# Quarter-array products and a planner with new durations in a fused attention kernel

## The chip, the core and the metric

The kernel runs on one core of a Trainium2 chip. The metric is the device time of one execution in microseconds (us); times are medians of several executions, and the profile is of one execution. The engines are named as in the profile: PE is TensorE (its weight loads are PEld), DVE is VectorE, ACT is ScalarE, POOL is GpSimd, SP is SyncE.

## The reference

One block of multi-head attention, in bfloat16: 2048 rows, 448 columns, 16 heads of 28 columns.

```python
B, S, D, H = 1, 2048, 448, 16          # x: (B,S,D), wqkv: (D,3D), wo: (D,D)
Dh = D // H                            # 28
qkv = (x @ wqkv).reshape(B, S, 3, H, Dh).transpose(2, 0, 3, 1, 4)
q, k, v = qkv[0], qkv[1], qkv[2]
scores = jnp.einsum("bhqd,bhkd->bhqk", q, k) * (Dh ** -0.5)
p = softmax(scores, axis=-1)
o = jnp.einsum("bhqk,bhkd->bhqd", p, v)
return o.transpose(0, 2, 1, 3).reshape(B, S, D) @ wo
```

## The kernel before

**Tiles.** The heads form four groups (`g`) of four; each head takes 32 of the 128 partitions (28 of its own, the rest for a softmax bound, the sums and padding). The queries form four chunks (`c`) of 512 columns. One pair of group and chunk is a set; there are 16. In a set, each of the 4 heads has 16 key tiles of 128 keys, so 64 half-steps: scores of one head, one key tile and 512 queries. There are 1024 half-steps in all.

**What one half-step does.** TensorE makes the scores from 32 (or, zero padded, 64) rows (L678, "S"; row tiles of the array, `32*128` or `64*128` in the profile), into one half of a PSUM pair `a0`/`a1` or into a single bank `d0`, `d1` or `m`. Pairs go to ScalarE, whose exponential covers two half-steps at once (128x1024, L864, `pt<-a`). Single ones go to VectorE, which makes the exponential by integer arithmetic (L879, `I<-d`), and for every four of them two further terms (L902, `J<-I`). TensorE then multiplies with V: products of 128 rows by 32 columns, one for each head, four of them side by side in the four column strips of the array (L962, `128*32`). Four such quarters are called a wave here. A half-step of ScalarE needs one quarter, one of VectorE three. All quarters of a set accumulate in the bank `o`, which VectorE copies out (L991); the sums are inverted and spread by DMAs, and GpSimd multiplies (L1013).

**The side work of TensorE.** Projections of K and Q are made in quarters of 32 columns too (L270, `112*32`). The rest uses the whole array: the norms of K and Q behind the softmax bound (L314, L477: `sq` times a mask, 512 columns), the projection of V (L513: 224 columns, four contraction chunks for each half-job), the output projection (L547, L1146 for the last chunk, L1213 at the very end: 448 columns), and products with zeros that fill idle time (L708 into the open bank `o`, L711 into a free bank). All but the last set's outputs pass through the bank `m`, which VectorE empties.

**The planner.** The order of instructions on each engine is made in Python when the program is built. The planner keeps a time for each engine, always advances the engine that is earliest, and picks its next piece of work by rules (`pick_pe`, `pick_act`, `pick_dve` and so on), with durations that are written in the code. On the chip every engine then takes its list in order and waits where data or a bank is not there. What matters here:

- `do_s` emits the scores for the next exponential as soon as their PSUM pair is free, with up to two single half-steps for VectorE; `do_sd` emits single half-steps alone.
- `s_deadline` is the time by which the next scores must begin so that ScalarE does not wait; other work of TensorE (`do_pv` for waves, the jobs of `add("PE", ...)`, `dense` for zero products) is picked only if it ends by then, with 0.1 us of tolerance.
- `D_S` is the duration of scores, `D_WAVE` of a wave, `D_SWITCH` a charge for each piece of other work; `D_EXP` is the duration of an exponential. `LATS` and `LAT` are the latencies from engine to engine. `SLOW_V` stretches all durations of VectorE by 3%.
- `dve_ok` decides whether a half-step goes to VectorE, by comparing when VectorE would be done with when ScalarE would be.

```python
D_S = 0.325
D_WAVE = 0.2135
D_SWITCH = 0.11
D_EXP = 0.912
# dense(): a zero product
return t + D_SWITCH + D_WAVE
# do_pv(): one or two waves
end = t + D_SWITCH + D_WAVE * len(ws)
```

Of the kernel before, what the change touches and what calls it, by code (L numbers as in the profile page):

```python
# [17 lines left out]
LATS = {("ACT", "PE"): 0.32, ("PE", "ACT"): 0.12, ("PE", "DVE"): 0.15, ("DVE", "PE"): 0.2}  # L18
D_S = 0.325
D_WAVE = 0.2135  # L20
D_SWITCH = 0.11
D_EXP = 0.912
SLOW_V = 1.03
D_SOON = 0.0
URGENT = 100
S_LEAD = 0.44


class Op:
    def __init__(self, eng, dur, emit, need=(), gives=(), pri=0, acq=None, rel=None, gate=0, lag=0.0, land=0.0,  # L30
                 cols=0, port=False):
        self.eng, self.dur, self.emit = eng, dur * (SLOW_V if eng == "DVE" else 1.0), emit
        self.need, self.gives, self.pri = list(need), list(gives), pri
        self.acq, self.rel, self.gate, self.lag, self.land, self.cols, self.port = acq, rel, gate, lag, land, cols, port
# [3 lines left out]
def kernel(  # L38
# [178 lines left out]
    cur = {"s": 0, "u": 0, "o": None, "oset": 0, "pv": 0, "half": 0, "o_open": False}  # L217
# [24 lines left out]
    def run(op, t):  # L242
# [3 lines left out]
        end = t + op.dur  # L246
        if op.port:
            port[op.eng] = end
# [4 lines left out]
        if isinstance(op.rel, tuple):  # L253
            parts.setdefault(op.rel[0], []).append(end + LAT)
            if len(parts[op.rel[0]]) == op.rel[1]:
                res[op.rel[0]] = max(parts.pop(op.rel[0]))
        elif op.rel is not None:
            res[op.rel] = end + LAT
# [6 lines left out]
    def mm_proj(ps, t, g, c, ccs):  # L265
        for cc in ccs:
            for i in range(HG):
# [4 lines left out]
                                 tile_position=(0, HP * i))  # L272

# [12 lines left out]
    def k_job(g, sc, bank, pri, gate=0, split=2):  # L286
# [14 lines left out]
        for p in range(split):  # L301
            add("PE", n * D_WAVE + (D_SWITCH if split > 1 else 0.02), lambda p=p: mm(p), pri=pri, gate=gate, cols=448 * n,
# [3 lines left out]
        add("POOL", 1.05, lambda: square(key, KAt[(g, sc)][:]), need=[key], gives=[("ksq", g, sc)], pri=pri, port=True)  # L306

    def kn_job(g, bank, pri, gate=0):
        key = ("KN", g)

        def mm(sc):
            if sc == 0:
                held[key] = bank_tile(bank) if bank[0] != "a" else pair_tile(bank)
            nc.tensor.matmul(out=held[key][:, 0:QW], lhsT=maskK[:, sc, :], rhs=sqt.pop(("K", g, sc))[:],  # L314
                             start=(sc == 0), stop=(sc == NQC - 1))
# [13 lines left out]
        for sc in range(NQC):  # L329
            add("PE", D_WAVE + 0.05, lambda sc=sc: mm(sc), pri=pri, gate=gate, cols=512,  # L330
# [5 lines left out]
    def k_first(sc, bank, nbank, eng, sq_eng, pri, late=False):  # L336
# [47 lines left out]
        add("PE", CC * D_WAVE + 0.02, mm, pri=pri, cols=448 * CC, acq=bank,  # L384
# [16 lines left out]
    def q_job(g, c, bank, pri, gate=0, split=2):  # L401
# [25 lines left out]
        for p in range(split):  # L427
            add("PE", n * D_WAVE + (D_SWITCH if split > 1 else 0.02), lambda p=p: mm(p), pri=pri, gate=gate, cols=448 * n,
# [7 lines left out]
        else:  # L436
            add("POOL", 1.05, lambda: square(key, QAt[(g, c)][:]), need=[key], gives=[("qsq", g, c)], pri=pri, port=True)
# [33 lines left out]
    def qn_job(g, cs, bank, pri, gate=0):  # L471
        key = ("QN", g, cs[0])

        def mm(k):
            if k == 0:
                held[key] = bank_tile(bank)
            nc.tensor.matmul(out=held[key][:], lhsT=maskK[:, cs[k], :], rhs=sqt.pop(("Q", g, cs[k]))[:],  # L477
                             start=(k == 0), stop=(k == len(cs) - 1))
# [16 lines left out]
        for k in range(len(cs)):  # L495
            add("PE", D_WAVE + 0.05, lambda k=k: mm(k), pri=pri, gate=gate, cols=512,
                need=[("qsq", g, cs[k]), ("km", g)] + ([key + (k - 1,)] if k else []), gives=[key + (k,)],
                acq=bank if k == 0 else None)
        add("DVE", 0.94, bound, need=[key + (len(cs) - 1,)], gives=[("su",) + key], rel=bank, pri=pri, port=True)
# [3 lines left out]
    def v_job(h, kt, bank, pri, gate=0, eng="DVE"):  # L503
# [4 lines left out]
        def mm(part):  # L508
# [3 lines left out]
            for cc in range(CC):  # L512
                nc.tensor.matmul(out=held[key][:, part * w:(part + 1) * w], lhsT=XT[b][cc // 2][:, cc % 2, t * P:(t + 1) * P],  # L513
                                 rhs=WRAW[2][:, cc, h * w:(h + 1) * w], start=(cc == 0), stop=(cc == CC - 1))
# [9 lines left out]
        for p in range(2):  # L524
            add("PE", 4 * 0.105 + D_SWITCH, lambda p=p: mm(p), pri=pri, gate=gate, cols=4 * 196,
# [14 lines left out]
    def oproj_job(c, tq, pri):  # L540
        key = ("O", c, tq)

        def mm(part):
            if part == 0:
                held[key] = bank_tile("m")
            for g in (2 * part, 2 * part + 1):
                nc.tensor.matmul(out=held[key][:, 0:D], lhsT=otile(g, c)[:, tq * P:(tq + 1) * P], rhs=WO[:, g, :],  # L547
                                 start=(g == 0), stop=(g == G - 1))
# [8 lines left out]
        for p in range(2):  # L557
            add("PE", 2 * 0.19 + D_SWITCH, lambda p=p: mm(p), pri=pri, cols=2 * D,
                need=[("OT", g, c) for g in range(G)] + ([key + (p - 1,)] if p else []), gives=[key + (p,)],
                acq="m" if p == 0 else None)  # L560
        add("DVE", 0.56, evac, need=[key + (1,)], gives=[key], rel="m", pri=pri)
# [144 lines left out]
    def dense(t, to):  # L706
        if to == "o" and cur["o_open"]:
            nc.tensor.matmul(out=cur["o"][:], lhsT=zero[:, 0:P], rhs=zero[:], start=False, stop=False,  # L708
                             skip_group_check=True)
# [3 lines left out]
        return t + D_SWITCH + D_WAVE  # L713
# [66 lines left out]
    def put_d(got):  # L780
        end = 0.0
        for b, pd, step, ch, n, t in got:
            end = max(end, t + D_S)
# [44 lines left out]
    def s_deadline():  # L828
# [3 lines left out]
        if len(exps) == 0:  # L832
            return max(r, free["ACT"] - S_LEAD)
        nxt = max(free["ACT"], exps[0][0]) + D_EXP * len(exps)
        return max(r, nxt - S_LEAD)

    def do_s(t):
# [16 lines left out]
        res[bank] = None  # L854
        end = t + D_S
# [20 lines left out]
    def do_a(t):  # L876
# [3 lines left out]
        end = t + 0.6 * SLOW_V  # L880
        res[b] = end + LAT
# [3 lines left out]
        pending.append({"step": step, "k": 0, "ap": dst.bitcast(BF16), "ready": end + LAT, "pt": None, "ch": ch})  # L885
# [12 lines left out]
    def do_add(t):  # L898
# [4 lines left out]
        end = port["DVE"] = t + (m * QW * 0.00026 + 0.068) * SLOW_V  # L903
        for n in range(m):
            pending.append({"step": ch["steps"][n], "k": k, "ap": r[:, n * QW:(n + 1) * QW].bitcast(BF16),
                            "ready": end + LAT, "pt": None, "ch": ch})
# [38 lines left out]
    def do_pv(t, ws):  # L945
# [7 lines left out]
        end = t + D_SWITCH + D_WAVE * len(ws)  # L953
# [25 lines left out]
    def finish_set(s, end):  # L979
# [37 lines left out]
        add("DVE", 0.26, recip, need=[("den", s)], gives=[("rec", s)], pri=50, port=True)  # L1017
# [30 lines left out]
    def pick_pe(t):  # L1048
# [8 lines left out]
        if main and left() and t + D_S + 0.1 <= dl:  # L1057
# [8 lines left out]
        ws = full[:2]  # L1066
        if len(ws) < 2 and (last_chance or op is None):
            ws = ws + rest[:2 - len(ws)] if last_chance else ws
        backlog = len(full)
        d_pv = D_SWITCH + D_WAVE * len(ws)  # L1070
        pv_ok = ws and (len(ws) >= 2 or last_chance) and t + d_pv <= dl + 0.1
# [189 lines left out]
```

## Time and profile before

| what | value |
|---|---|
| median of 3 executions | 370.25 us (370.12 to 370.31) |
| the profiled execution's own time | 370.24 us |
| its span, first to last instruction | 368.4 us |
| granted TensorE clock, mean | 0.999 |
| busy PE, DVE, ACT | 349.5, 347.3, 350.4 us |
| first exponential starts, last one ends | 19.08 us, 359.8 us |

Busy time is the union of the recorded instructions of an engine. Products are pipelined and the record of one goes on after the next has begun, so start-to-start times tell more than durations. The granted clock is given in tenths for 40 slices of the span (PEclk). "Idle before" is the time in which an engine had nothing running, with who ended it behind the arrow.

### The profile page before, as it was taken

Reading aid. Unit: us, or ns where it says so; the run is one execution under the profiler, and the core shown is the slowest. Engines: PE = TensorE matmul, PEld = TensorE weight load, DVE = VectorE, ACT = ScalarE, POOL = GpSimd, SP = SyncE. Lnnn points to the kernel's source line nnn. Section 1 sums busy time; section 2 is a strip of 40 time slices with the busy share of each in tenths; the row PEclk is TensorE's granted clock in tenths of the full one; section 3 lists DMA queues with packets and bytes.
Section 4 is the critical chain, followed back from the end, with each engine's and each line's share of the span. In section 5 each row is a group of like instructions: output and inputs, shape, how many; then the busy total and the mean of one; then the engine's idle time right before and its main releaser. Section 6 shows DMA issues by size and latency. Waiting matters only on the chain.

```text
span 368.4 us, 8926 instructions
## 1 busy us (share of the span) xinstructions
PE 349.5 (95%) x3522; PEld 111.6 (30%) x3522; DVE 347.3 (94%) x632; ACT 350.4 (95%) x384; POOL 72.7 (20%) x95
## 2 busy tenths in 40 slices
PE   8899999999999999999999999998898999999995
PEld 4443322222333233232222222222222222222222
DVE  7799999998999999999999999999999999999973
ACT  4599999999999999999999999999999999999991
POOL 8931033242010511221011314201010101010010
PEclk9999999999999999999999999999999999999999
DMA  8510010011001000010000002100000001010101
GB/s 254 126 39 12 3 29 31 8 41 36 6 29 32 2 4 28 22 52 16 29 3 9 23 4 59 24 16 18 24 8 10 25 27 55 26 56 27 42 16 50
DMA packets 15058, 12.18 MB, mean 33 GB/s; under 512 B 6812, under 2 KB 13096, under 8 KB 15016
## 3 DMA queue, kind: packets, MB, share of 16 engines
q1 hardware_dynamic: 13464, 10.19, 9.7%
q10 hardware_dynamic: 1040, 1.02, 0.9%
q8 instruction: 27, 0.44, 0.5%
q0 software_dynamic: 512, 0.40, 0.5%
q14 instruction: 15, 0.12, 0.1%
HBM read 7.58 MB, written 1.96 MB: 26 GB/s over the span
## 4 chain that ended last, share of the span: by engine, by line
PE 52%; ACT 30%; DVE 10%; issue 6%; DVEq 0%; ACTq 0%
ACT pt L864 30%; PE a L678 19%; PE o L962 16%; PE m L270 7%; DVE I L879 4%; DVE J L902 4%; PE m L547 1%; PE m L513 1%; PE o L595 1%; PE o L708 1%; PE d L678 1%; PE m L314 1%; DVE osb L552 1%; PE d L573 1%; PE a L270 1%
## 5 line engine op out<-in xcount | busy, mean ns | idle before, releaser
L864 ACT ACTIVATE pt<-a 128x1024 bf16<-128x1024 f32 x368 | 339.2, 1125 | 1.1 <-PE a L678 0.4
L879 DVE TENSOR_SCALAR I<-d 128x512 int16<-128x512 f32 x260 | 170.1, 682 | 5.3 <-PE d L678 3.9
L678 PE MATMUL a<-QP,KA 32*128 32x512 bf16 (+1 forms) x726 | 141.6, 381 | 11.2 <-ACT pt L864 10.1
L962 PE MATMUL o<-pt,VA 128*32 128x512 bf16 x736 | 105.5, 385 | 0.0
L902 DVE TENSOR_SCALAR J<-I 128x2048 int16<-128x2048 int16 x144 | 102.5, 744 | 0.2
L678 PEld LDWEIGHTS <-KA 32*128 32x128 bf16 (+1 forms) x1024 | 48.5, 91 | 145.4 <-issue 144.5
L678 PE MATMUL d<-QP,KA 32*128 32x512 bf16 x256 | 84.0, 384 | 0.4 <-DVE I L879 0.3
L962 PE MATMUL o<-J,VS 128*32 128x512 bf16 x576 | 78.7, 385 | 0.4 <-DVE J L902 0.4
L962 PE MATMUL o<-I,VA 128*32 128x512 bf16 x288 | 66.3, 386 | 0.1
L1013 POOL TENSOR_TENSOR xs<-o_sb,rr 128x512 bf16<-128x512 f32 x12 | 16.6, 1382 | 103.3 <-DMA rr<-scr 87.0
L962 PEld LDWEIGHTS <-VA 128*32 128x32 bf16 x1024 | 24.2, 94 | 36.7 <-issue 36.3
L280 POOL TENSOR_TENSOR sq<-QA 128x512 bf16<-128x512 bf16 x15 | 18.3, 1219 | 60.9 <-DVE QA L420 60.9
L270 PE MATMUL m<-XT,WRAW 112*32 112x512 bf16 x384 | 29.5, 384 | 0.0
L280 POOL TENSOR_TENSOR sq<-KA 128x512 bf16<-128x512 bf16 x12 | 13.2, 1102 | 59.2 <-DVE KA L298 59.2
L962 PEld LDWEIGHTS <-VS 128*32 128x32 bf16 x576 | 18.1, 94 | 19.7 <-issue 19.7
L879 DVE TENSOR_SCALAR I<-m 128x512 int16<-128x512 f32 x28 | 19.0, 679 | 0.1
L513 PE MATMUL m<-WRAW,XT 112*128 112x224 bf16 x128 | 17.1, 261 | 0.2
L1013 POOL TENSOR_TENSOR OTL<-o_sb,rr 128x512 bf16<-128x512 f32 x3 | 4.1, 1367 | 56.3 <-DMA rr<-scr 56.3
L708 PE MATMUL o<-zero 128*128 128x512 bf16 x40 | 13.5, 386 | 0.0
L513 PEld LDWEIGHTS <-XT 112*128 112x128 bf16 x128 | 10.2, 97 | 7.1 <-issue 7.1
L991 DVE COPY o_sb<-o 128x512 f32<-128x512 f32 x15 | 10.3, 684 | 1.4 <-PE o L962 1.3
L547 PE MATMUL m<-WO,xs 128*128 128x448 bf16 x36 | 10.9, 358 | 0.3 <-DVE I L879 0.2
(119 smaller groups left out, 195.8 us busy)
## 6 DMA issues: line engine op xcount, KB each, us to landing
rr<-scr SPq DMA_DIRECT2D x15, 256.0 KB
QP<-QA SPq DMA_DIRECT2D x60, 28.0 KB
out_dram<-osb SPq DMA_DIRECT2D x12, 112.0 KB
WRAW<-in_wqkv_dram SPq DMA_DIRECT2D x3, 392.0 KB
xs<-in_x_dram ACTq DMA_DIRECT2D x4, 224.0 KB
xs<-in_x_dram SPq DMA_DIRECT2D x4, 224.0 KB
QP<-su SPq DMA_DIRECT2D x30, 2.0 KB
out_dram<-VS SPq DMA_DIRECT2D x2, 224.0 KB
```

The source lines that it names most:

```text
L270: nc.tensor.matmul(out=ps[HP * i:HP * (i + 1), :], lhsT=w[:, cc, h * Dh:h * Dh + HP], rhs=XT[c][cc // 2][:, cc % 2, :], start=(cc == 0), s ...
L280: nc.gpsimd.tensor_tensor(out=t[:], in0=src, in1=src, op=ALU.mult)
L513: nc.tensor.matmul(out=held[key][:, part * w:(part + 1) * w], lhsT=XT[b][cc // 2][:, cc % 2, t * P:(t + 1) * P], rhs=WRAW[2][:, cc, h * w: ...
L547: nc.tensor.matmul(out=held[key][:, 0:D], lhsT=otile(g, c)[:, tq * P:(tq + 1) * P], rhs=WO[:, g, :], start=(g == 0), stop=(g == G - 1))
L678: nc.tensor.matmul(out=out_ap, lhsT=KAt[(g, j // XB)][r, (j % XB) * P:(j % XB + 1) * P], rhs=q[r, :], start=True, stop=True, tile_position ...
L708: nc.tensor.matmul(out=cur["o"][:], lhsT=zero[:, 0:P], rhs=zero[:], start=False, stop=False, skip_group_check=True)
L864: nc.scalar.activation(out=pt[:], in_=ps[:], func=ACT.Exp, scale=LN2 / 128.0)
L879: nc.vector.tensor_scalar(out=dst, in0=pd[:], scalar1=BIAS, scalar2=0.0, op0=ALU.add, op1=ALU.max)
L902: nc.vector.tensor_scalar(out=r[:, w], in0=ch["I"][:, w], scalar1=float(SHIFT[k]), scalar2=None, op0=ALU.add)
L962: nc.tensor.matmul(out=o[HP * i:HP * (i + 1), :], lhsT=vt[:, j % XB, gg, HP * i:HP * (i + 1)], rhs=e["ap"], start=(SETMM[key] == 1), stop= ...
L991: nc.vector.tensor_copy(out=st["o_sb"][:], in_=o[:])
L1013: nc.gpsimd.tensor_tensor(out=otile(g, c), in0=st["o_sb"][:], in1=st["rr"][:], op=ALU.mult)
```

## The change

A new helper makes a product over the whole array as four quarters, each with 32 of the 128 weight columns, at the four column strips. It is used for the norms in `kn_job` and `qn_job`, the projections of V, all output projections, and the zero product into the open bank `o`. The transposes, the norms of the first group (`k_first`, `qn_first`) and the zero product into a free bank stay as they were.

The planner's numbers are replaced, the charge `D_SWITCH` is gone, and a turn is charged in its place: scores begin at the earliest `D_TURN` after the last product in column form (`cur["c_end"]`). Waves are picked one at a time instead of two. The 3% on VectorE is gone, and the latency to TensorE after a release is taken from `LATS`.

```diff
-LATS = {("ACT", "PE"): 0.32, ("PE", "ACT"): 0.12, ("PE", "DVE"): 0.15, ("DVE", "PE"): 0.2}
-D_S = 0.325
-D_WAVE = 0.2135
-D_SWITCH = 0.11
-D_EXP = 0.912
-SLOW_V = 1.03
+LATS = {("ACT", "PE"): 0.165, ("PE", "ACT"): 0.167, ("PE", "DVE"): 0.13, ("DVE", "PE"): 0.145}
+D_S = 0.323
+D_TURN = 0.143
+D_WAVE = 0.226
+D_EXP = 0.904
+TOL = 0.1
-S_LEAD = 0.44
+S_LEAD = 0.49
...
+    def quarters(out, lhsT, rhs, start, stop, **k):
+        for i in range(P // HP):
+            r = slice(HP * i, HP * (i + 1))
+            nc.tensor.matmul(out=out[r, :], lhsT=lhsT[:, r], rhs=rhs, start=start, stop=stop, tile_position=(0, HP * i), **k)
...
# qn_job (kn_job, v_job, oproj_job, early_jobs and the last products alike)
-            nc.tensor.matmul(out=held[key][:], lhsT=maskK[:, cs[k], :], rhs=sqt.pop(("Q", g, cs[k]))[:],
-                             start=(k == 0), stop=(k == len(cs) - 1))
+            quarters(held[key][:], maskK[:, cs[k], :], sqt.pop(("Q", g, cs[k]))[:], k == 0, k == len(cs) - 1)
...
# durations of the jobs
-            add("PE", D_WAVE + 0.05, lambda k=k: mm(k), pri=pri, gate=gate, cols=512,
+            add("PE", D_WAVE, lambda k=k: mm(k), pri=pri, gate=gate, cols=512,
-            add("PE", 4 * 0.105 + D_SWITCH, lambda p=p: mm(p), pri=pri, gate=gate, cols=4 * 196,
+            add("PE", 4 * 0.1, lambda p=p: mm(p), pri=pri, gate=gate, cols=4 * 196,
-            add("PE", 2 * 0.19 + D_SWITCH, lambda p=p: mm(p), pri=pri, cols=2 * D,
+            add("PE", 2 * 0.192, lambda p=p: mm(p), pri=pri, cols=2 * D,
...
# dense: zero products
-            nc.tensor.matmul(out=cur["o"][:], lhsT=zero[:, 0:P], rhs=zero[:], start=False, stop=False,
-                             skip_group_check=True)
+            quarters(cur["o"], zero[:, 0:P], zero[:], False, False, skip_group_check=True)
...
-        return t + D_SWITCH + D_WAVE
+        return t + D_WAVE + (0.0 if main_on() else 0.1)
...
# s_deadline, and the start of scores in do_s and put_d
-        return max(r, nxt - S_LEAD)
+        return max(r, nxt - S_LEAD) - D_TURN
+
+    def turn(t):
+        return max(t, cur["c_end"] + D_TURN)
...
# VectorE's scores and terms
-        end = t + 0.6 * SLOW_V
-        res[b] = end + LAT
+        end = t + 0.6
+        res[b] = end + LATS[("DVE", "PE")]
...
# pick_pe
-        if main and left() and t + D_S + 0.1 <= dl:
+        if main and left() and turn(t) + D_S <= dl + D_TURN:
...
-        ws = full[:2]
-        if len(ws) < 2 and (last_chance or op is None):
-            ws = ws + rest[:2 - len(ws)] if last_chance else ws
         backlog = len(full)
-        d_pv = D_SWITCH + D_WAVE * len(ws)
-        pv_ok = ws and (len(ws) >= 2 or last_chance) and t + d_pv <= dl + 0.1
...
-        op_ok = op is not None and t + op.dur <= dl + 0.1
+        ws = full[:1] if full or not last_chance else rest[:1]
+        inside = cur["c_end"] > t - 0.02
+        pv_ok = ws and t + D_WAVE <= dl + TOL and (inside or backlog >= 2 or last_chance)
+        op_ok = op is not None and t + op.dur <= dl + TOL
...
-        if to is not None and (left() if main else t > 5.5) and t + D_SWITCH + D_WAVE <= dl and load_of(t) < WARM \
-                and (main or nxt is None or nxt > t + 0.25):
+        if to is not None and (left() if main else t > 5.5) and t + D_WAVE + 0.1 <= dl and load_of(t) < (WARM if main else 0.8) \
+                and (main or nxt is None or nxt > t + 0.34):
```

The smaller numbers of other jobs change as well (a square on GpSimd 1.05 to 1.15, the bound of Q on VectorE 0.94 to 0.88, a reciprocal 0.26 to 0.16, the copy of an output 0.56 to 0.535).

## The prediction

> **What bounds the kernel now.** I read the page first, then the timeline of TensorE period by period, then the groups by shape, and last the order of instructions of both programs. From the page:
>
> ```profile
> PE 349.5 (95%) x3522; PEld 111.6 (30%) x3522; DVE 347.3 (94%) x632; ACT 350.4 (95%) x384; POOL 72.7 (20%) x95
> L864 ACT ACTIVATE pt<-a 128x1024 bf16<-128x1024 f32 x368 | 339.2, 1125 | 1.1 <-PE a L678 0.4
> L678 PE MATMUL a<-QP,KA 32*128 32x512 bf16 (+1 forms) x726 | 141.6, 381 | 11.2 <-ACT pt L864 10.1
> PEclk9999999999999999999999999999999999999999
> ```
>
> Three engines are about 95% busy. ScalarE's 368 exponentials of 128x1024 set the rhythm. In the trace they follow each other at 0.904 us in 242 of 367 cases and never closer. 368 x 0.904 is 332.7 us, but from the first start (19.08) to the last end (359.8) it takes 340.7. The idle column (1.1 us) hides this, because a late exponential is recorded as a long one: its mean is 1125 ns. Listing the starts more than 0.954 apart gives 40 late places with 6.62 us above 0.904 in all. Only two of them (0.82 us) are copies of V on ScalarE itself. In the others a scores product came late, so I look at TensorE:
>
> ```profile
> 201.03 0.39 PE L678 MATMUL a<-QP,KA 32*128 32x512 bf16 x2
> 201.04 0.39 PE L678 MATMUL d<-QP,KA 32*128 32x512 bf16 x1
> 201.36 0.62 PE L270 MATMUL m<-XT,WRAW 112*32 112x512 bf16 x8
> 201.95 0.39 PE L678 MATMUL a<-QP,KA 32*128 32x512 bf16 x2
> ```
>
> This is an ordinary period: scores (row tiles), then two waves of four quarter products (column tiles), then scores again. Median start-to-start times over the trace: scores to what follows 0.322, wave to wave of one form 0.226, last wave to scores 0.363. That is 0.911 for a period with two waves, level with ScalarE's 0.904. Two score banks let TensorE lag: scores begin at the earliest 0.16 after an exponential's start, and the next exponential starts 0.49 after the scores it needs. So it stays on time while the scores begin within 0.41, a float of 0.25. Now the norms:
>
> ```profile
> 88.94 0.39 PE L678 MATMUL a<-QP,KA 32*128 32x512 bf16 x2
> 88.95 0.39 PE L678 MATMUL d<-QP,KA 32*128 32x512 bf16 x2
> 89.27 0.39 PE L477 MATMUL m<-sq,maskK 128*128 128x512 bf16 x1
> 89.59 0.40 PE L962 MATMUL o<-J,VS 128*32 128x512 bf16 x4
> 89.92 0.39 PE L678 MATMUL a<-QP,KA 64*128 64x512 bf16 x2
> ```
>
> A full-array product and one wave: 0.98, because full array to column tiles takes 0.32 where column to column takes 0.226. The array's turn costs 0.094. The same holds for output projections: 0.282 to the following wave against 0.20 to their own kind. Of the 40 late places, 28 (3.66 us) hold such a turn; ten (2.14 us) do not, most of them a product waiting in TensorE's queue for VectorE.
>
> **The change part by part.** *Turns.* Between the first and the last scores the old order has 38 turns between full array and column tiles. In the new order all norms, V and output projections and the zero products of that stretch have column form, and 4 such places are left, at its start. Per turn 0.094 (0.082 for output projections), together 3.4 us of TensorE. On the path is only what lies in late places: the smaller of 0.09 and the lateness, summed over the 28, is 2.2. I take -2.2; ends 0 (float hides them) and -3.4.
>
> *Exponentials.* The order has 366 instead of 368: 2 x 0.904 = -1.8. The four half-steps go to VectorE: four more of L879 and two more of L902, 0.60 apart each, 3.6 us. VectorE is 328.1 busy of 340 between 20 and 360, so 11.9 idle cover it; uncovered it would cost up to +3.6. Value 0. GpSimd's and SyncE's instructions and DMAs are as many as before.
>
> *The planner's numbers.* Old: scores 0.325 + switch 0.11 + two waves of 0.2135 = 0.862 per ordinary period, where the rows give 0.911. New: 0.143 + 0.323 + 0.452 = 0.918. Its new latencies also equal rows: exponential's start to scores 1.069 (0.904 + 0.165), scores to VectorE 0.453 (0.323 + 0.13). So it should no longer put scores later than it believes. Prices of the heavy periods from the rows, over 0.904: old order 12 of norm and wave (0.10), 11 of two output products and wave (0.26), five of two waves and norm (0.33), nine smaller or single ones, 7.6 in all; new order 11 of three waves (0.23), nine of output products and wave (0.18), some ten of other kinds, 6.2 in all, while norm and wave falls to 0.01. The float and light periods absorb most. For the ten late places without a turn, and new ones, I take -1.0 of their 2.14; ends -2.1 and, if the packing adds as much as it removes, +1.1.
>
> *Quarters of short products.* Each V product of 224 columns becomes four. Old price per contraction chunk:
>
> ```profile
> L513 PE MATMUL m<-WRAW,XT 112*128 112x224 bf16 x128 | 17.1, 261 | 0.2
> L573 PE MATMUL d<-ident,xs 128*112 128x128 bf16 x32 | 2.3, 225 | 0.0
> 362.38 0.64 PE L1203 MATMUL a<-identf,rT 128*32 128x128 f32 x16
> ```
>
> L513 start to start is 0.096. No row has four quarters of 224. Below: they stream at once, 0.096, nothing lost. Above: the densest quarters here are L1203, 16 in 0.64 less one duration of 0.27, or 0.109 from one four to the next: +0.013. Nothing speaks for a gain. A half-job (16 quarters) is 0.38 to 0.44; with scores and turns 0.85 to 0.90, inside 0.904, so 0 on the path; over 30 half-jobs at most 0.4 us. The far row is L573, one pair of weight load and product each 0.055; see the first rival. Quarters of 448 and 512 columns have the price of the waves.
>
> The page "TensorEngine Tiling (Array Packing)" of the Trainium skill, section Restrictions and Gotchas, says that column tiling loses the fast weight load; "TensorE: Matmul & The Clock Gate" of the Trainium skill, section LDWEIGHTS, gives columns / 1.2 ns, 27 ns for a quarter, an estimated 0.107 per four. By these pages, all of it on the path, 120 chunks would add 1.3 us to the sum; L1203's 0.109 agrees with the price, not with its being on the path.
>
> *Ends.* Before the main loop a norm product (about 0.25 with its turn) now stands ahead of the second K projection, and one zero product is gone (0.22): -0.1 to +0.3, value +0.15. After the last wave three early output products (3 x 0.2) now stand between L1203 and L1213, where TensorE had waited 0.3 for VectorE: 0 to +0.3, value +0.1. Zero products fall from 40 to 20 fours; they fill idle time, so 0; if the granted clock fell for it, PEclk would show it.
>
> **Sum.** The profiled execution took 370.24 (span 368.4 and 1.8 around it), the median being 370.25. 370.24 - 2.2 - 1.8 - 1.0 + 0.15 + 0.1 = **365.5**. Its own range is 363.0 (all turns, all late places) to 367.5 (half the turns, no late place gained).
>
> **Rivals.**
> 1. *Issue of quarters becomes the bound (slower).* V half-jobs are 16 weight loads and 16 products. If such pairs cannot follow faster than L573's 0.055, a half-job takes 0.88 and its period 0.32 + 0.88 + 0.14 = 1.34. That is 0.44 too long in some 25 periods, 11 us: 376.5. It decides once a four takes over about 0.11. Against it: L1203's quarters start 0.025 apart; but those 16 pairs had been waiting in the queue. The Trainium skill's "TensorE: Matmul & The Clock Gate", section Back-to-back issue gap, gives 81 ns for a sustained pair at 128 columns, which would be longer still; L573's 0.055 contradicts it here. Chance 0.09.
> 2. *No margin left.* The planner drops its 3% on VectorE and cuts VectorE to TensorE from 0.20 to 0.145 (the rows: 0.73 from start to start, 0.60 + 0.13). If its plan slips, the ten waits of 0.21 become thirty: +4.3 in place of -1.0, 370.8. Against it: the rows fit the new numbers within 0.02. Chance 0.13, half above 371.0.
> 3. *Float hides the turns.* Only the exponentials and ends count: 370.24 - 1.8 + 0.25 = 368.7. For it: two thirds of the exponentials are on time already. Chance 0.13.
> 4. *The turn stays* between quarters of different products (112 rows in one, 128 in the other; no row shows the two side by side): again 368.7, chance 0.03.
>
> **Numbers.** The forecast has 0.62. Faster by over 0.2% (0.74 us, about what a measurement of this kernel can tell from no change): 0.62 + 0.13 + 0.03 = 0.78. Same: half of rival 2, 0.07. Slower: the other half and rival 1, 0.15. The range takes in the forecast's own range but its lowest end, rivals 3 and 4 and the lower half of rival 2: 363.4 to 370.6.
>
> **What would show it.** Right: a norm and a wave between scores give a period near 0.91; norm to wave 0.226; V quarters 0.096 to 0.109 per four; 366 exponentials; from the first exponential to the last end about 336 us; late places with 2 to 3 us. Wrong: V half-jobs with periods over 1.0; many scores with idle time that VectorE ends; first exponential later than 19.5, or more than 9.2 us from the last exponential to the end; PEclk below 9.

## The result and the profile after

The changed kernel takes 369.25 us (median of 16 executions, 368.68 to 370.24), the kernel before 370.37 in the same session (369.52 to 371.09). The ratio is 0.9973, 95% interval 0.9963 to 0.9983: faster by 0.27%, about 1.1 us, where the sum forecast 4.7 (370.24 to 365.5). The profiled execution took 369.31 us, its span is 367.4 (368.4 before). From the page after:

```profile
PE 342.2 (93%) x4228; PEld 112.3 (31%) x4228; DVE 346.7 (94%) x638; ACT 347.9 (95%) x382; POOL 69.1 (19%) x95
L874 ACT ACTIVATE pt<-a 128x1024 bf16<-128x1024 f32 x366 | 336.9, 1153 | 1.4 <-PE a L682 1.1
L682 PE MATMUL a<-QP,KA 32*128 32x512 bf16 (+1 forms) x722 | 141.3, 381 | 15.1 <-ACT pt L874 14.1
PEclk9999999999999999999999999999999999999999
```

As the order said, 366 exponentials are left, and TensorE has 7 us less work. The granted clock is untouched. TensorE now waits longer for ScalarE (15.1 us in place of 11.2), so it has become freer. The mean of an exponential tells the rest: 1153 ns against 1125. Exponentials still come late, at fewer places and by more at each.

Nearly all turns are gone. The timeline of TensorE at the place of the prediction's second timeline:

```profile
88.87 0.39 PE L682 MATMUL a<-QP,KA 32*128 32x512 bf16 x2
88.88 0.39 PE L682 MATMUL d<-QP,KA 32*128 32x512 bf16 x2
89.69 0.40 PE L279 MATMUL m<-sq,maskK 128*32 128x512 bf16 x4 [0.43 <-DVE QA L426]
89.92 0.39 PE L972 MATMUL o<-J,VS 128*32 128x512 bf16 x4
90.24 0.39 PE L682 MATMUL a<-QP,KA 64*128 64x512 bf16 x2
```

From norm to wave it is 0.23 (0.32 before), from wave to scores 0.32. But the first norm waits 0.43 us for VectorE to empty the bank `m` (L426, a copy of Q), and the period is 1.37 us long. That is the new pattern: the product is cheap and stands in the queue.

A projection of V in quarters, in the same view:

```profile
24.33 0.41 PE L682 MATMUL a<-QP,KA 64*128 64x512 bf16 x2
24.76 0.57 PE L279 MATMUL m<-WRAW,XT 112*32 112x224 bf16 x16
25.14 0.40 PE L972 MATMUL o<-pt,VA 128*32 128x512 bf16 x2
```

Sixteen quarters take 0.38 us up to the next wave, 0.096 for each four, the price that the full-array products had.

With late places counted as before (starts of exponentials over 0.954 apart, what they have above 0.904):

| | before | after |
|---|---|---|
| exponentials | 368 | 366 |
| first exponential starts | 19.08 | 20.07 |
| late places: number, us | 40, 6.62 | 24, 6.00 |
| of these with a turn | 28, 3.66 | 2, 0.46 |
| without one (and not a copy of V on ScalarE) | 10, 2.14 | 20, 4.68 |
| all time above 0.904 | 7.94 | 7.66 |
| first exponential's start to last one's end | 340.7 | 338.7 |
| last end to end of span | 8.6 | 8.6 |

So 2.0 us are gained between the exponentials, of which 1.8 are the two that are gone, and 1.0 is lost in front of them. The late places with a turn have all but vanished, and as many microseconds without one have come.

**What they wait for.** Two of the 24 are copies of V (0.86 us) and nine are small (0.7 us together). The other thirteen, followed back to their releasers, are of four kinds. The first and largest, five places with 2.1 us: VectorE's second terms (J, L912) stand still beside GpSimd. One of them in the timeline, which lists several engines:

```profile
226.75 1.27 POOL L1023 TENSOR_TENSOR xs<-o_sb,rr 128x512 bf16<-128x512 f32 x1
226.76 1.81 DVE L912 TENSOR_SCALAR J<-I 128x2048 int16<-128x2048 int16 x1
228.50 0.68 DVE L889 TENSOR_SCALAR I<-d 128x512 int16<-128x512 f32 x1
229.23 0.37 PE L682 MATMUL d<-QP,KA 32*128 32x512 bf16 x1 [0.40 <-DVE I L889]
```

The term starts 0.01 us behind GpSimd's multiplication and ends 0.55 us after it, 1.81 us in place of 0.68: nearly all of its own work was done after the other had ended. VectorE's exponential (L889) behind it frees a bank too late, the scores wait 0.40 us, and ScalarE's exponential that starts at 230.57 is 0.73 late. "SBUF — State Buffer" of the Trainium skill, section Who interferes with whom, says that VectorE in its two-port modes and GpSimd exclude each other for a whole instruction, and that the one issued first wins; these rows agree.

The second kind, two places with 0.92 us: at 55.0 VectorE waits for the sums of a set (the gather DMA, L1006).

```profile
53.06 0.60 SPq L1006 DMA_DIRECT2D den<-o_sb  x1
53.76 2.10 SPq L498 DMA_DIRECT2D QP<-su  x4
54.98 0.25 DVE L1010 RECIPROCAL rec<-den 128x16 f32<-128x16 f32 x1 [0.92 <-DMA den<-o_sb]
57.03 0.37 PE L682 MATMUL d<-QP,KA 32*128 32x512 bf16 x1 [0.61 <-DVE I L889]
```

The gather was issued at 53.06, behind five DMAs of rows (QP<-QA) that SyncE had taken 3.98 us to issue; the planner counts four of them as 2.4 us. The third kind, 0.92 us in four places, is an exponential that waits for a buffer of `pt`. The fourth, 0.46 us in two places, is zero products into the free bank `m`, a pair at 258 us (0.40) and a single one at 279 (0.06). They are still full-array products; the prediction counted the zero products of this stretch as column form. The pair:

```profile
258.55 0.82 PE L714 MATMUL m<-zero 128*128 128x512 bf16 x2
259.30 0.40 PE L972 MATMUL o<-I,VA 128*32 128x512 bf16 x4
259.63 0.39 PE L682 MATMUL a<-QP,KA 32*128 32x512 bf16 x2
```

Both go into the same bank; together they take 0.75 us up to the next wave, where the planner counts 0.45.

**The start.** Before, ScalarE's square of the first part of K came first and VectorE's copy second; after, the other way round:

```profile
8.73 0.69 ACT L284 ACTIVATE sq<-a,kmask 128x512 bf16<-128x512 f32 x1 [0.43 <-PE a L270]
9.64 1.05 PE L270 MATMUL a<-XT,WG 112*32 112x512 bf16 x16
```

```profile
8.70 0.81 DVE L359 TENSOR_SCALAR KA<-a,kmask,ones 128x512 bf16<-128x512 f32 x1 [0.30 <-PE a L272]
9.55 0.69 ACT L291 ACTIVATE sq<-a,kmask 128x512 bf16<-128x512 f32 x1 [1.25 <-DVE KA L359]
10.29 0.38 PE L375 MATMUL a<-sq,blockK 128*128 128x512 bf16 x1 [0.61 <-ACT sq L291]
10.59 0.61 PE L272 MATMUL a<-XT,WG 112*32 112x512 bf16 x8
```

The first fence is of before, the second of after. The square waits for the copy (both read bank `a`), the norm for the square, and the second projection of K stands behind the norm: 10.59 in place of 9.64. Not all of the 1.0 us need come from the order: in the five profiles of the old order the first exponential starts at 18.88 to 19.43, in those of the new orders with this start at 19.86 to 20.59.

### The profile page after: what moved, and what is told of

It is laid out like the page before. It is cut to its first block, busy times and chain, and to the rows that moved or that the text cites. A ratio compares the mean times of both kernels' runs of the same rounds, so it can differ in the third digit from the quotient of the medians.

```text
span 367.4 us, 10365 instructions
## 1 busy us (share of the span) xinstructions
PE 342.2 (93%) x4228; PEld 112.3 (31%) x4228; DVE 346.7 (94%) x638; ACT 347.9 (95%) x382; POOL 69.1 (19%) x95
## 4 chain that ended last, share of the span: by engine, by line
ACT 43%; PE 33%; DVE 14%; issue 9%; DMA 1%; DVEq 0%; ACTq 0%
ACT pt L874 42%; PE a L682 11%; PE o L972 9%; DVE I L889 6%; PE m L272 4%; DVE J L912 3%; PE m L279 2%; PE o L599 1%; DVE VA L527 1%; PE d L682 1%; DVE QA L426 1%; DVE VS L537 1%; PE a L272 1%; DMA den<-o_sb 1%; PE d L272 1%
## 5 line engine op out<-in xcount | busy, mean ns | idle before, releaser
L874 ACT ACTIVATE pt<-a 128x1024 bf16<-128x1024 f32 x366 | 336.9, 1153 | 1.4 <-PE a L682 1.1
L889 DVE TENSOR_SCALAR I<-d 128x512 int16<-128x512 f32 x262 | 170.5, 680 | 4.7 <-PE d L682 4.4
L682 PE MATMUL a<-QP,KA 32*128 32x512 bf16 (+1 forms) x722 | 141.3, 381 | 15.1 <-ACT pt L874 14.1
L972 PE MATMUL o<-pt,VA 128*32 128x512 bf16 x732 | 104.2, 384 | 0.1
L912 DVE TENSOR_SCALAR J<-I 128x2048 int16<-128x2048 int16 x146 | 101.6, 723 | 0.2
L682 PE MATMUL d<-QP,KA 32*128 32x512 bf16 (+1 forms) x257 | 82.7, 384 | 1.1 <-DVE I L889 1.0
L972 PE MATMUL o<-I,VA 128*32 128x512 bf16 x292 | 64.7, 385 | 0.2
L1023 POOL TENSOR_TENSOR xs<-o_sb,rr 128x512 bf16<-128x512 f32 x12 | 16.0, 1336 | 101.0 <-DMA rr<-scr 57.9
L287 POOL TENSOR_TENSOR sq<-QA 128x512 bf16<-128x512 bf16 x15 | 16.3, 1087 | 66.9 <-DVE QA L426 66.9
L889 DVE TENSOR_SCALAR I<-m 128x512 int16<-128x512 f32 x30 | 20.3, 678 | 0.1
L279 PE MATMUL m<-WRAW,XT 112*32 112x224 bf16 x512 | 17.8, 261 | 0.1
L1023 POOL TENSOR_TENSOR OTL<-o_sb,rr 128x512 bf16<-128x512 f32 x3 | 3.8, 1271 | 56.4 <-DVE I L889 19.6
L279 PEld LDWEIGHTS <-XT 112*32 112x32 bf16 x512 | 10.5, 96 | 7.4 <-issue 7.1
L279 PE MATMUL m<-WO,xs 128*32 128x448 bf16 x156 | 12.3, 358 | 0.2 <-DVE I L889 0.2
L682 PE MATMUL m<-QP,KA 32*128 32x512 bf16 (+1 forms) x30 | 11.5, 384 | 0.1
```

The source lines that it names most:

```text
L279: nc.tensor.matmul(out=out[r, :], lhsT=lhsT[:, r], rhs=rhs, start=start, stop=stop, tile_position=(0, HP * i), **k)
L287: nc.gpsimd.tensor_tensor(out=t[:], in0=src, in1=src, op=ALU.mult)
L682: nc.tensor.matmul(out=out_ap, lhsT=KAt[(g, j // XB)][r, (j % XB) * P:(j % XB + 1) * P], rhs=q[r, :], start=True, stop=True, tile_position ...
L874: nc.scalar.activation(out=pt[:], in_=ps[:], func=ACT.Exp, scale=LN2 / 128.0)
L889: nc.vector.tensor_scalar(out=dst, in0=pd[:], scalar1=BIAS, scalar2=0.0, op0=ALU.add, op1=ALU.max)
L912: nc.vector.tensor_scalar(out=r[:, w], in0=ch["I"][:, w], scalar1=float(SHIFT[k]), scalar2=None, op0=ALU.add)
```

## The experiments

Each was timed in five rounds beside the kernel before on the same chip (its medians: 370.12 to 370.63). Ratios are to that kernel.

**The two halves of the change.** First the new planner with full-array products:

```diff
# e2_full_new_order, against the changed kernel
-        for i in range(P // HP):
-            r = slice(HP * i, HP * (i + 1))
-            nc.tensor.matmul(out=out[r, :], lhsT=lhsT[:, r], rhs=rhs, start=start, stop=stop, tile_position=(0, HP * i), **k)
+        nc.tensor.matmul(out=out[:, :], lhsT=lhsT, rhs=rhs, start=start, stop=stop, **k)
```

> The order of the changed kernel, but every product that the change makes in quarters is one product over the whole array again. Theory A: the turns come back into an order that was planned without them; late places with a turn add 2 to 3.5 us to the changed kernel, 371 to 372.7 us, slower than the kernel before. Theory B: 369.2, as the changed kernel.

Measured: 371.22 us, ratio 1.0034 (1.0021 to 1.0046). That is in the range of theory A. Against the changed kernel's 0.9973 the turns cost 2.0 (medians) to 2.3 us (ratios) in the new order. Its profile has 39 late places with 9.17 us, against 24 with 6.00. So the new order, with full-array products, has 2.55 us more of late places than the old one (6.62), and the quarters take 3.2 of them away.

Then the old planner, and so the old order, with the same products in quarters as in the change:

```diff
# e1_quarters_old_order, against the kernel before (the other calls alike)
-            nc.tensor.matmul(out=held[key][:], lhsT=maskK[:, cs[k], :], rhs=sqt.pop(("Q", g, cs[k]))[:],
-                             start=(k == 0), stop=(k == len(cs) - 1))
+            quarters(held[key][:], maskK[:, cs[k], :], sqt.pop(("Q", g, cs[k]))[:], k == 0, k == len(cs) - 1)
```

> The order of the kernel before, with its old planner; only the products over the whole array are made as quarters. Theory A (turns cost what they seem to, and the new order gives the gain away elsewhere): the 3.66 us in late places with a turn fall to about 0.5, the ten others stay near 2.1, first exponential still at 19.1; 367.0 to 368.3 us, ratio 0.991 to 0.995. Theory B (the float between TensorE and ScalarE hides the turns): 369.8 to 370.4.

Measured: 372.92 us, ratio 1.0078 (1.006 to 1.0096), slower than either kernel. Neither expectation held. SyncE's queue, first before, then in this run:

```profile
54.08 0.47 SPq L1005 DMA_DIRECT2D scr<-rec  x1
55.63 0.60 SPq L1010 DMA_DIRECT2D rr<-scr  x1
56.32 2.10 SPq L493 DMA_DIRECT2D QP<-su  x4
```

```profile
54.75 0.48 SPq L1006 DMA_DIRECT2D scr<-rec  x1
57.92 0.60 SPq L1011 DMA_DIRECT2D rr<-scr  x1
58.61 2.09 SPq L496 DMA_DIRECT2D QP<-su  x4
```

The spread of the inverted sums (rr) can be issued when they have landed in DRAM (scr). That took 1.55 us before and 3.17 here, and the bounds of Q (QP<-su) stand behind it. The DMA records show what fell in between: from 55.8 to 56.85 a DMA engine moved 16 KB of instructions. Such records follow TensorE's instruction count (27 of them with 3522 products before, 33 with 4299 here), so with quarters they fall elsewhere. What came of it, in TensorE's timeline:

```profile
62.87 0.39 PE L680 MATMUL d<-QP,KA 32*128 32x512 bf16 x1 [1.34 <-DMA QP<-su]
```

And in the table by stretches of the same run (length; busy us and count of PE, PEld, DVE, ACT, POOL; the granted clock; DMA share and GB/s):

```profile
63.00:63.60 0.60, 0.60 (x9) 0.12 (x8) 0.30 (x1) 0.00 (x0) 0.60 (x1) 1.00 0.00 0
64.50:66.00 1.50, 1.50 (x15) 0.24 (x11) 0.87 (x3) 1.01 (x2) 1.04 (x1) 0.50 0.00 0
67.20:67.70 0.50, 0.50 (x8) 0.12 (x6) 0.03 (x1) 0.30 (x1) 0.00 (x0) 1.00 0.00 0
```

The scores wait 1.34 us, and from about 63.7 to 67.1 the granted clock is 0.5. Late places of 1.85, 0.61 and 0.54 us follow. They are not all of this run's loss: at 23.7 and 24.5 us scores also wait 0.32 and 0.41 us for rows of Q (QP<-QA), which they do in no other run of this order; what delayed those rows was not followed.

**Moving the fetches.** To shift where they fall, the ten warm-up products at the very start are made in quarters as well, and nothing else differs from the run above:

```diff
-        nc.tensor.matmul(out=warm[:], lhsT=zero[:, 0:P], rhs=zero[:], start=True, stop=True)
+        quarters(warm, zero[:, 0:P], zero[:], True, True)
```

> The old order with quarters once more, and the ten zero products of the warm-up are quarters too: no new work on the path, but 60 more instructions at the start of TensorE's list, so that its 16 KB instruction fetches fall about 2.5 us earlier. Theory D (in the last run a fetch at 55.8 us held up the DMA of the inverted sums, SyncE's queue stood behind it, scores waited 1.9 us, and TensorE's clock fell to half for 3.4 us): the DMA from sums to spread takes 1.4 to 1.6 us instead of 3.2 in that place, the clock stays at 0.999, and the time falls from 372.9 to 367.8 to 369.2. Rival (the quarters themselves slow that order, or lower the activity that the clock gate sees): 372 to 374 again, clock 0.989 to 0.995.

Measured: 369.25 us, ratio 0.9972 (0.9957 to 0.9986), 3.7 us below the run above and 0.05 over the range of theory D; the first exponential starts at 19.43. At this place the sums now take 1.56 us from scr to rr, the clock stays full, and the late places add up to 5.78 us. So the old order with quarters is as fast as the changed kernel. Such a fetch need not cost anything: in the kernel before, scr to rr takes 3.15 and 2.78 us in two sets with one, and no scores wait for a DMA. In the changed kernel's own trace, scr to rr takes 1.44 to 1.50 in the twelve sets without a fetch in between, and 2.55, 2.53 and 2.22 in the three with one.

**The start again.** In the changed kernel the copies of the first two parts of K are put behind their squares again, and the first norm behind the second projection, as in the old order:

```diff
+            if not late and ("sqd", sc) not in held:
+                held[("ev", sc)] = evac
+                return
...
+            if sc == 0 and ("mmd", 1) not in held:
+                held[("nrm", 0)] = norm
+                return
```

> The changed kernel with the two swaps of its start undone: ScalarE's squares of the first two K chunks come before VectorE's copies of them again, and the first norm product after the second K projection. All later orders are those of the changed kernel. Theory A: first exponential at 19.1 to 19.3 instead of 20.07, total 368.2 to 368.5. Rival (the start is caught up later, because something else ends last): 369.0 to 369.4.

Measured: 369.23 us, ratio 0.9979 (0.9967 to 0.999), in the rival's range. The first exponential starts at 19.58 in place of 20.07 (19.1 to 19.3 were expected), but in the profile the late places rise from 6.00 to 6.82: what the start gives, later waits take back.

**GpSimd beside VectorE.** The multiplication of the outputs on GpSimd (L1023, 15 of them, 1.27 to 1.78 us) is cut to 64 of its 512 columns, in the new and in the old order:

```diff
-            nc.gpsimd.tensor_tensor(out=otile(g, c), in0=st["o_sb"][:], in1=st["rr"][:], op=ALU.mult)
+            nc.gpsimd.tensor_tensor(out=otile(g, c)[:, 0:64], in0=st["o_sb"][:, 0:64], in1=st["rr"][:, 0:64], op=ALU.mult)
```

> The changed kernel, but GpSimd's 15 multiplications take 64 of their 512 columns (the rest of the output is left out). Theory A (VectorE's second terms stand still while GpSimd multiplies, and the scores behind them come late): no second term of over 1.0 us beside a multiplication, late places without a turn fall from 4.7 to 2.5 to 3.2 us, total 367.3 to 368.2. Rival (VectorE's delays have another cause, such as the new latencies without margin): late places stay at 4.2 to 4.7, total 368.9 to 369.4.

> The kernel before, but GpSimd's 15 multiplications take 64 of their 512 columns (the rest of the output is left out), as was done to the changed kernel, where it was worth 1.0 us. If GpSimd's standing in VectorE's way costs both plans the same (theory C: it is a tax on any plan, not what ate this change's gain): 368.8 to 369.6, ratio 0.996 to 0.9985. If it eats the gain of the new plan alone (theory A): 369.9 to 370.5.

Measured: 368.27 us in the new order (ratio 0.9955, 0.9938 to 0.9971), 368.70 in the old one (0.9961, 0.9947 to 0.9975). The multiplications cost 0.7 (by the ratios) to 1.0 us (by the medians) in the new order and 1.4 to 1.9 in the old one. They are a price of both, not what took the gain from the new one alone (theory C of the second run, whose time came out 0.1 us under its range). The first run lies between its two ranges: as theory A said, no second term beside a multiplication takes over 1.0 us, but the late places fell only from 6.00 to 5.23. The time that second terms lose beyond 0.60 each (start to start, in VectorE's unbroken stretches) fell from 6.2 to 1.8 us. So most of it had not been on the path, and what is traced to GpSimd in a profile (2.1 us above, 1.6 of it with a multiplication) is not what its removal brings.

The same can be had with all the work done: squares and multiplications in four pieces of 128 columns.

```diff
+            for k in range(4):
+                w = slice(k * P, (k + 1) * P)
+                nc.gpsimd.tensor_tensor(out=otile(g, c)[:, w], in0=st["o_sb"][:, w], in1=st["rr"][:, w], op=ALU.mult)
```

> The changed kernel with GpSimd's squares and multiplications in four pieces of 128 columns; same results, same order. If VectorE gets its turn between two pieces, second terms beside GpSimd take at most 1.0 us instead of 1.4 to 1.7, and the late places behind them (468, 236, 150, 730 and 526 ns) shrink: 367.8 to 368.8 us. Rival (the pieces' own start costs make GpSimd so much longer that VectorE is met more often): 369.2 to 370.

Measured: 368.42 us, ratio 0.9945 (0.9933 to 0.9958), as expected. No second term is longer than 0.99 us any more (1.81 with whole instructions): VectorE waits for a piece, not for the whole.

> The pieces and the restored start together. If the two are independent: 0.5 us below the pieces alone, 367.3 to 368.3. If what the start gains is lost in other meetings of DMAs and VectorE, as it was without the pieces: the same as the pieces alone within 0.3 us.

Measured: 368.13 us, ratio 0.9938 (0.9922 to 0.9953); the first exponential starts at 19.32. This is 0.29 below the pieces alone and lies in both ranges, so it does not decide.

> The old order with products in quarters, the warm-up products in quarters too, and GpSimd's squares and multiplications in four pieces of 128 columns: what e7 is for the new order. Theory A (apart from the turns the new plan is worth nothing: its two exponentials less are given back at the start and in products that wait for VectorE): as fast as e7, 368.4 within 0.5 us. Theory B (the new plan is worth its two exponentials, 1.8 us, and only GpSimd's strokes hid it): slower than e7 by 1.3 to 2.0 us, 369.7 to 370.5.

Measured: 368.70 us, ratio 0.9956 (0.994 to 0.9972). Theory A held. This order has 368 exponentials and 3.91 us of late places; e7 has 366 and 5.52, and its first exponential starts 0.7 later. That is 1.8 saved and 2.3 given back in the profiles; the times are the same within their intervals.

**The margin on VectorE.**

```diff
-("DVE", "PE"): 0.145}
+("DVE", "PE"): 0.2}
+SLOW_V = 1.03
```

> The changed kernel, with the planner's old margin on VectorE put back and nothing else: 3% on all its durations, and 0.2 us from VectorE to TensorE in place of 0.145. Theory A (the dropped margin is why products wait in TensorE's queue, rival 2 of the prediction): the sum of the late places falls from 6.0 to under 5.0, the time to 367.8 to 368.5, even with 366 to 368 exponentials. Theory B (the late places come from VectorE's terms beside GpSimd, from a DMA and from buffers, which no 3% covers): the sum stays at 5.5 to 7.5 and the time at 368.8 to 370.

> e8 with the planner's old margin on VectorE as in e10. If the margin is what the new plan lacks, it gains on e8 what e10 gains on the changed kernel: 366.8 to 367.5. If not, 367.8 to 368.8.

Measured: 371.83 us (ratio 1.0044, 1.003 to 1.0058) and 370.24 (1.0002, 0.9993 to 1.0011), 2.6 and 2.1 us slower than without the margin, above every range of both expectations. The page of e10 says where:

```profile
L875 ACT ACTIVATE pt<-a 128x1024 bf16<-128x1024 f32 x370 | 340.1, 1162 | 1.2 <-PE a L683 1.0
```

With the margin the planner hands fewer half-steps to VectorE and makes 370 exponentials, 3.6 us more; the late places fall by 0.4 (e10) and 0.6 (e12) only. Dropping the margin was worth more than it cost. With eight half-steps fewer on VectorE than the changed kernel, the late places hardly move, which suggests that the four half-steps the change moved to VectorE explain little of them.

**Two numbers of the planner.** In e8, which has the start and the pieces:

```diff
-            add("SP", 2.4, rows, need
+            add("SP", 3.2, rows, need
-        return t + D_WAVE + (0.0 if main_on() else 0.1)
+        return t + (D_WAVE if to == "o" and cur["o_open"] else 0.445) + (0.0 if main_on() else 0.1)
```

> e8, with two of the planner's numbers set to what the trace shows: four DMAs of rows on SyncE take 3.2 us to issue and not 2.4, and a zero product into a free bank 0.445 and not 0.226. Theory A (single wrong numbers cost what the late places they explain cost): the wait for the sums at 55 us (0.9) and the pair of zero products at 258 us (0.4) go, and the time falls from 368.1 to 366.8 to 367.4. Theory B (another plan brings other late places in the same number): 367.7 to 368.8.

Measured: 366.51 us, ratio 0.99 (0.9885 to 0.9916), below both ranges: the fastest of all, and 2.7 us below the changed kernel. Its gather of the sums is issued earlier, with no wait for it on VectorE:

```profile
48.57 3.13 SPq L445 DMA_DIRECT2D QP<-QA  x4
51.80 0.60 SPq L1020 DMA_DIRECT2D den<-o_sb  x1
```

Both places are gone, the late places fall from 5.69 to 4.31. But is it these numbers, or simply another order? Each of them by itself in the changed kernel:

> The changed kernel with one number of the planner: four DMAs of rows take SyncE 3.2 us and not 2.4; the order is the same up to about 48 us. If the number is what costs: VectorE's wait for the sums at 55 us and the two late exponentials behind it (0.9 us) go, the sum of the late places falls from 6.0 to 4.7 to 5.2, the time to 367.9 to 368.6. If any other order would do as well or as badly: the one place goes and others come, 368.9 to 369.8.

> The changed kernel with one number of the planner: a zero product into a free bank takes 0.445 us and not 0.226; the order changes from the first exponentials on. If the number is what costs: the pairs of zero products behind the late places at 258.8 and 279 us (0.4 and 0.06) go, 368.6 to 369.0. If any other order would do as well or as badly: 368.9 to 369.9, with the late places elsewhere.

Measured: e13 370.80 us (ratio 1.0023, 1.0013 to 1.0033), e14 368.80 (0.9961, 0.9948 to 0.9973). e14 came as expected of a number that costs; e13 is above both of its ranges. With the truer time for the rows the wait at 55 us went, as meant, and the kernel became 1.5 us slower: 40 late places with 8.78 us. Its second terms lose about 9.5 us beyond 0.60 each, in the changed kernel 6.2. One such place in e13, then the same four terms with GpSimd in pieces (e15):

```profile
143.08 4.41 DVE L912 TENSOR_SCALAR J<-I 128x2048 int16<-128x2048 int16 x4
143.40 1.50 POOL L1023 TENSOR_TENSOR xs<-o_sb,rr 128x512 bf16<-128x512 f32 x1 [1.73 <-DMA rr<-scr]
144.86 1.48 POOL L287 TENSOR_TENSOR sq<-QA 128x512 bf16<-128x512 bf16 x1
```

```profile
142.25 3.01 DVE L914 TENSOR_SCALAR J<-I 128x2048 int16<-128x2048 int16 x4
142.85 3.14 POOL L1027 TENSOR_TENSOR xs<-o_sb,rr 128x128 bf16<-128x128 f32 x4 [1.11 <-DMA rr<-scr]
```

Four terms take 4.41 us beside two whole GpSimd instructions in a row ("strokes" in the expectations), 3.01 beside pieces. The multiplication starts when its DMA lands ("<-DMA rr<-scr"), not when the planner thinks. The planner does know the collision: it plans a second term only when GpSimd is through (`can_add = adds and port["POOL"] <= t`). But it does so by its own times. It lets a multiplication begin 6.0 us after the issue of the spread (0.5 and 5.5); in the changed kernel GpSimd, where it was free, began after 4.8 to 5.4. The change left these numbers as they were.

> e13 with GpSimd's squares and multiplications in four pieces of 128 columns, as in e7. If GpSimd's strokes on VectorE's second terms are what makes this order worse than the changed kernel's, the pieces gain far more here than the 0.83 us between the changed kernel and e7: from 370.8 to 367.8 to 368.6, with a sum of late places of 4.5 to 5.8. If the orders differ by themselves: 369.5 to 370.3, with a sum over 7.

> e14 with GpSimd's squares and multiplications in four pieces. If the strokes make the difference between orders, and the pair of zero products costs what its place shows: 0.3 to 0.5 us below e7, 367.9 to 368.2. If the orders differ by themselves: as far below e14 as e7 is below the changed kernel or less, 368.0 to 368.8.

Measured: e15 368.14 us (ratio 0.994, 0.9927 to 0.9952), e16 367.69 (0.9928, 0.9914 to 0.9942). The pieces take 2.7 us off e13, 1.1 off e14 and 0.8 off the changed kernel. With whole instructions the three orders lie 2.0 us apart (368.80 to 370.80), with pieces 0.7 (367.69 to 368.42). But e11, another new order with pieces, lies 1.2 us below the lowest of them, so three orders are too few to say that pieces make orders alike. In e15's late places the expectation missed (6.03 us, not under 5.8), in its time not; e16 is below both of its ranges.

## Why the prediction was right and wrong

By the terms of its sum, in the profiled executions (370.24 before, 369.31 after):

| term | forecast | measured |
|---|---|---|
| turns | -2.2 | -2.0 to -2.3 (e2 against the changed kernel) |
| two exponentials less | -1.8 | -1.8 (count; rhythm 0.904) |
| other late places | -1.0 | +1.9 |
| start | +0.15 | +1.0 |
| end | +0.1 | 0.0 |
| VectorE's 3.6 us | 0 | not separated; little (e10, e12) |
| quarters of V | 0 | 0.096 per four, as before |

The third value is what is left of the change in all time above 0.904 (7.66 - 7.94 = -0.28) when the turns have had their 2.2; counted directly, the places without a turn went from 2.14 to 4.68. The sum is about -1.1; the two spans differ by 0.97 us, the two executions by 0.93.

**Right.** The turns cost what the prediction said, -2.2 against -2.0 to -2.3, but part of this is luck. The 2.2 was worked out from the late places of the old order, and in that order the quarters brought less: 1.0 (ratio) to 1.4 us (medians) in e6, or 1.4 to 1.7 with the 0.35 by which its first exponential starts later. They brought the forecast sum in an order whose late places nobody had seen. Quarters of 224 columns stream at the lower bound, so rivals 1 and 4 fell. The Trainium skill's rule on the fast weight load ("TensorEngine Tiling (Array Packing)", Restrictions and Gotchas), for which the prediction gave 1.3 us, cost nothing that these runs show. Rival 3 fell with e2. The prediction's warning signs were named rightly: a first exponential later than 19.5, and scores that VectorE ends.

**Wrong: the other late places.** The failed step is "For the ten late places without a turn, and new ones, I take -1.0 of their 2.14", with "+1.1" as the worse end. They rose from 2.14 to 4.68, beyond the worse end. The step took the planner's better numbers for a better order on the chip. The runs show that the order itself gained nothing: with quarters in both, old order and new are the same within their intervals (e6 and the changed kernel; e9 and e7), although the new one has two exponentials less. That the quarter products are cheaper was passed on in full (e2), that the order is better was not.

Why the new places came is shown only in part. Nearly all of the new numbers are durations and latencies of TensorE, ScalarE and VectorE. The places traced above come in good part from numbers that stayed, the time at which GpSimd starts (a DMA sets it) and SyncE's issue times, and from one that got worse: a zero product into a free bank went from 0.32 to 0.23 in the plan, and a pair takes 0.75 on the chip. The step priced the old ones as "a product waiting in TensorE's queue for VectorE" without asking what VectorE was waiting for, although the trace of before had such collisions too (8.6 us lost by the second terms). But GpSimd's multiplications explain only 0.7 to 1.0 us here and more in the old order (e4, e5), and putting a single number right can make the kernel slower (e13). So the cause of the rest stays open.

**Wrong: the start.** The failed step is "-0.1 to +0.3, value +0.15". It counted TensorE's instructions and not the readers of bank `a`. The new plan puts VectorE's copy before ScalarE's square, and three engines follow each other where two ran side by side. The order of both engines could have been read before: the square now stands behind the copy. As e3 shows, its 1.0 us was not a loss of 1.0: half of it restored (0.49) brought nothing measurable, and 0.3 us with the pieces (e8 against e7), inside the intervals of both.

**Rival 2** ("no margin left") had the symptom, more waits for VectorE, but its remedy does not help: e10 and e12 show that the margin, put back, costs over 2 us and takes only 0.4 to 0.6 off the late places. It priced only the waits and not the exponentials that a margin adds.

**Still open.** The gain of e11 over e8 (1.6 us) is more than the two late places that its numbers explain (1.3), and e15 and e16 gain 0.3 and 0.7 on e7; how much of it is luck of one order was not separated. No run has put the planner's time for the spread right, which decides where GpSimd and VectorE meet. The effect of the fetches on the changed kernel itself was not measured either: three of its fifteen sums wait for one.

## What to carry to other kernels

When a planner gets better numbers, its plan gets tighter, and not for that better. First list what starts on the chip at another time than in the plan (here GpSimd's start, set by a DMA, and the DMA queue's issue time), and look for the collisions in the old trace. An engine that is 19% busy can hold up one that is 94% busy if its single instructions hold a shared resource. Cutting them into pieces cost only time of its own (GpSimd's busy time went from 69.1 to 101.5 us in e7) and gained 0.8 to 2.7 us. But a wait that a profile traces to one cause is not yet what its removal brings: test it. A removed cost is best priced only where it lies in a late place, and even then the price belongs to that order: here the same turns were worth 2.0 to 2.3 us in one order and 1.0 to 1.4 in the other.

## What the runs showed of the hardware

- A VectorE term of 0.68 us that meets a GpSimd instruction of 1.27 us ends 0.55 us after it (1.81 in all), which reads as a hold for the whole instruction and not as a slowdown. In pieces of 128 columns no term took over 0.99.
- With an instruction fetch of 16 KB, about 1 us long, in between, small DMAs came later: scr to rr 1.44 to 1.50 without one in the changed kernel, 2.2 to 2.6 with one, and 3.2 in e1. In e1 late places of 3.0 us followed such a wait; moving the fetches made the kernel 3.7 us faster (e6), not all of it by this wait. Longer times have another cause as well: in the set of e6 that took 3.94, SyncE issued four DMAs of rows (3.25 us) between the two.
- After scores that had waited 1.34 us the granted clock fell to 0.5 for 3.4 us. "TensorE: Matmul & The Clock Gate" of the Trainium skill, section What's actually happening, speaks of a free-running window of about 3.4 us; the length agrees, but TensorE had been idle for less than one window.
- Between products of different column-tiled shapes (128 rows and 112 rows) no turn shows: 224-column quarters to the next wave 0.096, norm to wave 0.23.
